# Loading and taking w1's last columns ahead of w3's in layer 0's feed-forward

## The chip, the cores and the metric

The kernel runs on one core of a Trainium2 chip. The metric is device time in microseconds, the median of three runs. Besides it there is one execution taken by the hardware profiler, whose rows are shown below; times in rows are microseconds from the start of that execution's span.

## The reference

Two identical layers in float32 on a batch of 4 tokens (one per sequence, width 512). Each layer is an attention block with a key and value cache and a gated feed-forward, both with a layernorm ahead and a residual add behind:

```python
x = x + A(layernorm(x), k_cache, v_cache, wq, wo)   # 32 query heads, 8 key/value heads, 4096 positions, width 128
x = x + B(layernorm(x), w1, w3, w2)

def B(x, w1, w3, w2):                # w1, w3: 512 x 1792, w2: 1792 x 512
    gate = x @ w1
    up = x @ w3
    return (silu(gate) * up) @ w2
```

Both layers use the same caches and weights. That is why so many bytes pass: the caches are loaded once per layer, less what is kept on chip between the layers.

## The kernel before, in words

All inputs lie in one array `rows` of 128 partitions, in the order in which they are used. On chip one large tile, `space`, holds everything loaded. It is divided into 218 places of 256 columns (1 KB per partition, 128 KB for the whole place). A list written out by hand, `LOADS` (line 54), gives every load: first place in the stream, number of places, place in `space`. The function `pump` (line 123) goes through that list in order. It issues a load only when all places of its destination are free, and stops at the first one that is not; `done` (line 158) frees a tile's places once the instructions that read it are written and calls `pump` again. So loads never overtake each other. All go out on SyncE (SP), whose queue is in order as well: at run time SP waits for the readers of the old tile, issues, and goes on to the next load. Each load is spread over the core's 16 DMA engines.

Layer 0 goes through the eight head groups in order and layer 1 in reverse, so that some tiles of the turn can be kept. For each group TensorE multiplies queries with keys (line 349), VectorE and ScalarE make the softmax, and TensorE multiplies with values (line 413). Then comes the feed-forward (function `feed_forward`, line 480).

There the columns are cut in two: "a" is the first 256 of each quarter, "b" the remaining 192. The weight tiles are w1a and w1b, w3a and w3b, each in four parts k = 0 to 3 (the contraction over 512 is cut into four). `part(bank, kind, ks)` (line 484) does the 16 matmuls of each of its parts as 4 per k and frees the part's tile behind them (w1 is not freed in layer 0, since layer 1 uses the loaded copy again). `swish` (line 504) is the sigmoid on ScalarE and a product on VectorE, `times_up` (line 508) the product with the other bank, `turn_h` (line 511) the transposes, `down` (line 528) the 14 tiles of w2. `hum` (line 496) issues filler matmuls on TensorE whose result is not used.

In layer 0 the places of these tiles are chained:

```
w3a      144 to 160        w1a   0 to 16         w1b  16 to 28
w3b 0    161 to 164        w3b 1 145 to 148      w3b 2 148 to 151     w3b 3 151 to 154
w2 0-1   154 to 158        w2 2-3 160 to 164     w2 4 158 to 160      w2 5-6 144 to 148
w2 7     148 to 150        w2 8-9 150 to 154
```

So w3b 0 needs room that a stored half tile frees (function `store_half`, line 213), w3b 1 to 3 need w3a's parts to be consumed, w2's second load (tiles 2 and 3) needs w3b 0 to be consumed, and the next ones w3a, w3b 1, w3b 2 and w3b 3.

Of the kernel before, what the change touches and what calls it, by code (L numbers as in the profile page):

```python
# [61 lines left out]
    (868, 8, 72), ("half", 0, 186), (876, 4, 188), (880, 8, 192), ("stash", 1, 202), (888, 8, 206),  # L62
# [15 lines left out]
def tile_decode_layers(ctx: ExitStack, tc: tile.TileContext, rows, out):  # L78
# [76 lines left out]
    def loaded(*key):  # L155
        return place(where[key], size[key[0]])

    def done(layer, *key):
        if layer == 0 and (key[0][:2] == "w1" or key[0] in ("wq", "wo") and key[1] >= HELD or key[:2] == ("kv", TURN) and key[2] in KEPT or key[0] == "w2" and key[1] >= LASTS):
            return  # L160
        at, n = where[key], size[key[0]]
        if key == CUT:
            half = where["half"]
            taken[half:half + n // 2] = [False] * (n // 2)
            at, n = at + n // 2, n // 2
        taken[at:at + n] = [False] * n
        pump()
# [18 lines left out]
    part = work.tile([P, 32], F32, name="part", tag="p", bufs=1)  # L186
# [33 lines left out]
    def scores():  # L220
        return psum.tile([P, BLOCK], F32, name="scores", tag="scores")
# [258 lines left out]
    def feed_forward(layer, xT, factor):  # L480
        gate, up = o_ps if layer else o_ps[::-1]
        cols = {"a": slice(0, HALF), "b": slice(HALF, FJ)}

        def part(bank, kind, ks=range(KC)):
            s = cols[kind[2]]
            for k in ks:
                w = loaded(kind, k).rearrange("p (j f) -> p j f", j=4)
                for j in range(4):
                    nc.tensor.matmul(bank[32 * j:32 * j + 32, s], xT[:, 32 * k:32 * k + 32], w[:, j],  # L489
                                     start=(k == 0), stop=(k == KC - 1))  # L490
                done(layer, kind, k)

        def old_x():
            nc.tensor.matmul(x_ps, ident, x_sb, start=True, stop=False)

        def hum(at, n):
            nc.tensor.matmul(pt[:, at:at + n, :], ident, ident.unsqueeze(1).to_broadcast([P, n, P]),
                             start=True, stop=True)

        h = work.tile([P, FJ], F32, name="h", tag="p", bufs=1)  # L500
        hT = work.tile([P, 14, B], F32, name="hT", tag="pT", bufs=1)
        pt = scores().rearrange("p (n s) -> p n s", n=NT)

        def swish(s):
            nc.scalar.activation(h[:, s], gate[:, s], AF.Sigmoid, scale=rstd[:, 0:1])
            nc.vector.scalar_tensor_tensor(h[:, s], gate[:, s], rstd[:, 0:1], h[:, s], op0=ALU.mult, op1=ALU.mult)

        def times_up(s):
            nc.vector.scalar_tensor_tensor(h[:, s], up[:, s], rstd[:, 0:1], h[:, s], op0=ALU.mult, op1=ALU.mult)

        def turn_h(u):
            if u == 0:
                for i in range(2):
                    nc.tensor.transpose(pt[:, i, :], h[:, i * P:(i + 1) * P], ident)
                nc.vector.tensor_copy(hT[:, 0:8, :],
                                      pt[:, 0:2, :].rearrange("p i (j b) -> p (i j) b", j=4)[:, :, 0:B])
            else:
                nc.tensor.transpose(pt[:, 2, :], h[:, 2 * P:3 * P], ident)
                nc.tensor.transpose(pt[:, 3, :], h[:, FJ - P:FJ], ident)
                nc.tensor.transpose(pt[0:64, 3, :], h[:, FJ - 64:FJ], ident)  # L520
                nc.vector.tensor_copy(hT[:, 8:12, :],
                                      pt[:, 2, :].rearrange("p (j b) -> p j b", j=4)[:, :, 0:B])
                last = pt[:, 3, :].rearrange("p (j u b) -> p j u b", j=2, u=2)
                for i in range(2):
                    nc.vector.tensor_copy(hT[64 * i:64 * i + 64, 12:14, :],
                                          last[64 * i:64 * i + 64, :, i, 0:B])

        def down():
            order = (*range(8), *range(LASTS, 14), *range(8, LASTS)) if layer else range(14)
            for n, m in enumerate(order):  # L530
                t = loaded("w2", m)
                for k in range(KC):
                    nc.tensor.matmul(x_ps[32 * k:32 * k + B, :], hT[:, m, :], t[:, k * P:(k + 1) * P],  # L533
                                     start=False, stop=(n == 13))
                done(layer, "w2", m)
                if layer == 0 and m in (1, 3, 8, 11):
                    hum(2 if m < 5 else 0, 1)
                if m == (1 if layer else 5):
                    turn_h(1)

        if layer == 0:
            part(up, "w3a", (0,))
            factor()
            part(up, "w3a", range(1, KC))
            old_x()
            hum(1, 3)
            part(gate, "w1a")
            part(up, "w3b", (0, 1))
            swish(cols["a"])
            times_up(cols["a"])  # L550
            hum(2, 2)
            turn_h(0)
            hum(2, 2)
            part(gate, "w1b")
            swish(cols["b"])
            nc.scalar.activation(spare, half[:, 0:1], AF.Exp)
            part(up, "w3b", (2, 3))
            times_up(cols["b"])
            hum(2, 1)
        else:  # L560
            old_x()
            part(gate, "w1a", (0,))
            factor()
            part(gate, "w1a", range(1, KC))
            part(gate, "w1b")
            swish(slice(0, FJ))
            part(up, "w3a")
            times_up(cols["a"])
            part(up, "w3b")
            turn_h(0)  # L570
            times_up(cols["b"])
        down()

    for layer in range(LAYERS):
# [54 lines left out]
        busy(BUSY[2])  # L629
        xT, factor = layernorm()  # L630
        feed_forward(layer, xT, factor)
    assert state['next'] == len(LOADS)
    nc.vector.tensor_copy(x_sb, x_ps)
# [47 lines left out]
```

## Time and profile before

| | |
|---|---|
| Median of three runs | 703.02 us (703.0 to 704.46) |
| Span of the profiled execution | 701.4 us, 1.6 us below that median |
| TensorE matmul busy | 421.4 us, 60% of the span |
| VectorE, ScalarE busy | 144.6 us (21%), 43.2 us (6%) |
| Moved by DMA | 297.34 MB, 424 GB/s over the span |
| DMA in the chain that ended last | 72% |

The profiled execution's own time is known by its span alone; 703.02 is the median of runs apart from it. In the page's slices of the span the DMA engines are at 9 tenths or more in 39 of 40. A DMA row counts an issue from where SP takes it up to where its instruction ends; the transfer itself comes later and is told by the time to landing. A landing is the moment at which all 16 engines have delivered their parts.

### The profile page before, as it was taken

To read this page: it belongs to the slowest core of one execution; us is meant where nothing else is said; L and a number is where in the kernel's file an instruction comes from. 1 tells how busy PE (TensorE), PEld (TensorE's weight loads), DVE (VectorE), ACT (ScalarE), POOL (GpSimd) and SP (SyncE) were. 2 spreads that over 40 slices of the span, in tenths; PEclk is the share of its full clock that TensorE was granted. 3 is DMA by queue.
4 is the path that set the end of the run, shared out by engine and by line. 5 is a ranking of instruction groups with operands and counts; after the bars stand their busy time and mean duration, and the time that the engine had idled before them with its cause. 6 is when DMAs were issued, how large, how long until landed. Compare 5 with 4: busy or idle time off the path is not lost.

```text
span 701.4 us, 7509 instructions
## 1 busy us (share of the span) xinstructions
PE 421.4 (60%) x3282; PEld 134.3 (19%) x3282; DVE 144.6 (21%) x512; ACT 43.2 (6%) x106; POOL 3.0 (0%) x10
## 2 busy tenths in 40 slices
PE   1266466644774529677687996544554725557677
PEld 0121121211221103121134231101111201112224
DVE  2012112121030203230221332102111401211322
ACT  0010000100000001010111210000100001000100
POOL 0000000000000000000000000000000000000000
PEclk9997677866698578886999998877867968778989
DMA  9999999999999999999999999999999999999996
GB/s 411 430 420 422 460 427 419 431 449 426 422 425 455 418 438 416 431 431 428 419 388 399 418 433 435 448 427 420 451 426 428 444 415 439 430 442 416 425 421 274
DMA packets 12847, 297.34 MB, mean 424 GB/s; under 512 B 1424, under 2 KB 1552, under 8 KB 4624
## 3 DMA queue, kind: packets, MB, share of 16 engines
q1 hardware_dynamic: 12816, 296.88, 98.9%
q8 instruction: 25, 0.41, 0.2%
q14 instruction: 6, 0.05, 0.0%
HBM read 296.81 MB, written 0.07 MB: 423 GB/s over the span
## 4 chain that ended last, share of the span: by engine, by line
DMA 72%; PE 24%; DVE 1%; another core or an unknown queue 1%; issue 1%; ACT 1%; SPq 1%; DVEq 0%; ACTq 0%
DMA space<-in_rows 72%; PE scores L349 12%; PE o L413 6%; PE sums_ps L330 1%; PE turned L374 1%; PE sums_ps L319 1%; PE o L489 1%; PE scores L230 0%; SPq L149 0%; ACT p L367 0%; DVE acc L361 0%; PE stored L467 0%; PE sums_ps L446 0%; PE sums_ps L457 0%
## 5 line engine op out<-in xcount | busy, mean ns | idle before, releaser
L349 PE MATMUL scores<-space,qT 128*32 128x512 f32 x1024 | 167.9, 712 | 137.6 <-DMA space<-in_rows 136.9
L413 PE MATMUL o<-space,pT 128*16 128x512 f32 x1024 | 152.5, 712 | 102.3 <-DMA space<-in_rows 92.0
L349 PEld LDWEIGHTS scores<-space,qT 128*32 128x32 f32 x1024 | 35.2, 122 | 213.6 <-issue 171.9
L413 PEld LDWEIGHTS o<-space,pT 128*16 128x16 f32 x1024 | 31.9, 109 | 201.2 <-issue 95.0
L361 DVE TENSOR_REDUCE acc<-scores 128x1 f32<-128x512 f32 x32 | 22.1, 691 | 184.8 <-PE scores L349 184.8
L367 ACT ACTIVATE p<-scores,acc 128x512 f32<-128x512 f32 x30 | 20.6, 687 | 557.2 <-DVE acc L361 420.4
L436 DVE SCALAR_TENSOR_TENSOR o<-o,acc,o 128x128 f32<-128x128 f32 x112 | 39.3, 351 | 44.4 <-PE o L413 41.0
L376 DVE COPY pT<-turned 128x256 f32<-128x256 f32 x32 | 13.6, 425 | 163.0 <-PE turned L374 163.0
L374 PE MATMUL turned<-ident,p 128*128 128x128 f32 x128 | 22.8, 305 | 11.3 <-ACT p L367 11.3
L374 PEld LDWEIGHTS turned<-ident,p 128*128 128x128 f32 x128 | 14.6, 150 | 45.2 <-ACT p L367 25.4
L319 PE MATMUL sums_ps<-space,xT 128*32 128x512 f32 x120 | 20.9, 718 | 2.7 <-DMA space<-in_rows 2.7
L447 DVE COPY o<-sums_ps 128x16 f32<-128x16 f32 x16 | 2.8, 174 | 93.0 <-PE sums_ps L446 93.0
L330 PEld LDWEIGHTS sums_ps<-same,shares 128*128 128x128 f32 x120 | 17.3, 222 | 16.9 <-DVE shares L325 11.9
L330 PE MATMUL sums_ps<-same,shares 128*128 128x4 f32 x120 | 18.6, 278 | 0.9 <-DVE shares L325 0.9
L489 PE MATMUL o<-space,xT 128*32 128x192 f32 (+1 forms) x256 | 13.5, 355 | 1.9 <-DVE xT L248 1.2
L467 PE MATMUL stored<-space,o 128*32 128x512 f32 x104 | 13.5, 592 | 0.0
L325 DVE TENSOR_SCALAR shares<-sums_ps,columns 128x512 f32<-128x512 f32 x15 | 11.1, 743 | 1.7 <-PE sums_ps L319 1.7
L533 PE MATMUL sums_ps<-space,hT 128*4 128x128 f32 x224 | 9.0, 273 | 3.8 <-DMA space<-in_rows 3.5
L235 PE MATMUL o<-columns,same 128*32 128x1 f32 x64 | 2.0, 181 | 14.5 <-DVE columns L579 13.5
L446 PEld LDWEIGHTS sums_ps<-columns,o 128*128 128x128 f32 x32 | 5.8, 227 | 19.9 <-issue 14.0
L489 PEld LDWEIGHTS o<-space,xT 128*32 128x32 f32 x256 | 7.5, 110 | 6.8 <-DVE xT L248 1.4
L446 PE MATMUL sums_ps<-columns,o 128*128 128x16 f32 x32 | 7.3, 306 | 0.6 <-DVE o L436 0.6
(105 smaller groups left out, 143.3 us busy)
## 6 DMA issues: line engine op xcount, KB each, us to landing
space<-in_rows SPq DMA_DIRECT2D x7, 4096.0 KB, 25.3
space<-in_rows SPq DMA_DIRECT2D x3, 6144.0 KB, 31.1
space<-in_rows SPq DMA_DIRECT2D x8, 2048.0 KB, 24.8
space<-in_rows SPq DMA_DIRECT2D x2, 7168.0 KB, 43.5
space<-in_rows SPq DMA_DIRECT2D x4, 3072.0 KB, 26.0
space<-in_rows SPq DMA_DIRECT2D x11, 1024.0 KB, 14.2
space<-in_rows SPq DMA_DIRECT2D x3, 3584.0 KB, 16.7
space<-in_rows SPq DMA_DIRECT2D x2, 5120.0 KB, 20.6
```

The costliest lines, as they stand in the source:

```text
L319: nc.tensor.matmul(wide[32 * k:32 * k + 32, :], xT[:, 32 * k:32 * k + 32], w[:, k, :], start=True, stop=True)
L330: nc.tensor.matmul(misc[:, h * B:(h + 1) * B], shares[:, h * DH:(h + 1) * DH], same[:, 0:B], start=True, stop=True)
L349: nc.tensor.matmul(ps[32 * b:32 * b + 32, :], qT[:, b, at:at + 32], u, start=(m < 2), stop=(m >= TILES - 2))
L361: nc.vector.tensor_reduce(acc[:, i:i + 1], ps, axis=AX.X, op=ALU.max, negate=True)
L367: nc.scalar.activation(p.rearrange("p n s -> p (n s)"), ps, AF.Exp, bias=acc[:, i:i + 1], scale=1.0 if scale is None else scale, accum_out ...
L374: nc.tensor.transpose(pt[:, n, :], p[:, n, :], ident)
L376: nc.vector.tensor_copy(pT, pt.rearrange("p n (b r) -> p n b r", b=B)[:, :, :, 0:ROW])
L413: nc.tensor.matmul(o_ps[i][32 * b:32 * b + ROW, :], pT[:, r // 2, b, :], t[:, j * NB * DH:(j + 1) * NB * DH], start=(r < 2), stop=(r >= TI ...
L436: nc.vector.scalar_tensor_tensor(o, o_ps[s][:, j * DH:(j + 1) * DH], acc[:, 16 + NB * s + j:17 + NB * s + j], o, op0=ALU.mult, op1=ALU.add)
L446: nc.tensor.matmul(misc[:, 0:B * REP], o, head, start=True, stop=True)
L467: nc.tensor.matmul(bank[32 * h:32 * h + 32, :], oT[:, h, :], w[:, h, :], start=first, stop=last)
L489: nc.tensor.matmul(bank[32 * j:32 * j + 32, s], xT[:, 32 * k:32 * k + 32], w[:, j], start=(k == 0), stop=(k == KC - 1))
```

## The change

Two things are moved, and no work is added or left out. In `LOADS` the load of w1b, (1168, 12, 16), moves ahead of those of w3b 0, (1196, 3, 161), and w3b 1, (1199, 3, 145). In layer 0's feed-forward the 16 matmuls on w3b 0 and 1 move from behind those on w1a to behind those on w1b, `swish` of the last columns and a small activation.

```diff
-    (1180, 16, 144), (1152, 16, 0), (1196, 3, 161), (1199, 3, 145), (1168, 12, 16), (1202, 3, 148), (1205, 3, 151),
+    (1180, 16, 144), (1152, 16, 0), (1168, 12, 16), (1196, 3, 161), (1199, 3, 145), (1202, 3, 148), (1205, 3, 151),
...
             part(gate, "w1a")
-            part(up, "w3b", (0, 1))
             swish(cols["a"])
             times_up(cols["a"])
             hum(2, 2)
...
             part(gate, "w1b")
             swish(cols["b"])
             nc.scalar.activation(spare, half[:, 0:1], AF.Exp)
+            part(up, "w3b", (0, 1))
             part(up, "w3b", (2, 3))
             times_up(cols["b"])
```

## Rows read from the trace of the kernel before

**Rows 1.** DMA queues on the page: packets, MB, share of 16 engines' span.

```profile
q1 hardware_dynamic: 12816, 296.88, 98.9%
q8 instruction: 25, 0.41, 0.2%
```

**Rows 2.** The chain that ended last: shares, then pieces (start, us, what).

```profile
DMA 72%; PE 24%; DVE 1%; another core or an unknown queue 1%; issue 1%; ACT 1%; SPq 1%; DVEq 0%; ACTq 0%
...
365.90 8.20 DMA space<-in_rows
...
375.77 6.79 DMA space<-in_rows
...
689.06 8.85 DMA space<-in_rows
```

**Rows 3.** Windows: busy PE, PEld, DVE, ACT, POOL; clock, DMA share, GB/s.

```profile
361.50:365.50 4.00, 3.19 (x54) 1.71 (x52) 1.02 (x7) 0.00 (x0) 0.55 (x1) 1.00 0.71 250
364.00:364.50 0.50, 0.50 (x16) 0.21 (x8) 0.00 (x0) 0.00 (x0) 0.44 (x1) 1.00 0.34 107
364.50:365.00 0.50, 0.50 (x10) 0.30 (x3) 0.00 (x0) 0.00 (x0) 0.00 (x0) 1.00 0.83 160
365.50:366.00 0.50, 0.50 (x6) 0.16 (x8) 0.00 (x0) 0.00 (x0) 0.00 (x0) 1.00 1.23 424
```

**Rows 4.** SP's issues: w1a, w3b 0, w3b 1, w1b, w2 2-3, 4, 7.

```profile
342.44 0.33 SPq L149 DMA_DIRECT2D space<-in_rows  x1
360.34 0.33 SPq L149 DMA_DIRECT2D space<-in_rows  x1
363.48 0.33 SPq L149 DMA_DIRECT2D space<-in_rows  x1
363.86 0.42 SPq L149 DMA_DIRECT2D space<-in_rows  x1
...
368.09 0.33 SPq L149 DMA_DIRECT2D space<-in_rows  x1
368.47 0.44 SPq L149 DMA_DIRECT2D space<-in_rows  x1
...
372.79 0.33 SPq L149 DMA_DIRECT2D space<-in_rows  x1
```

**Rows 5.** DMA view, us to landing: w1a, w3b 0, w3b 1, w1b, w2 2-3, 4.

```profile
space<-in_rows SPq DMA_DIRECT2D x1, 2048.0 KB, 22.7
space<-in_rows SPq DMA_DIRECT2D x1, 384.0 KB, 5.8
space<-in_rows SPq DMA_DIRECT2D x1, 384.0 KB, 3.7
space<-in_rows SPq DMA_DIRECT2D x1, 1536.0 KB, 7.0
space<-in_rows SPq DMA_DIRECT2D x1, 512.0 KB, 7.3
space<-in_rows SPq DMA_DIRECT2D x1, 256.0 KB, 8.2
```

**Rows 6.** A window at the kernel's end, columns as in rows 3.

```profile
695.50:696.00 0.50, 0.50 (x24) 0.49 (x21) 0.00 (x0) 0.00 (x0) 0.00 (x0) 1.00 0.64 225
```

**Rows 7.** TensorE's timeline: w3b 0-1, transposes, filler, w1b, w3b 2.

```profile
367.52 0.83 PE L489 MATMUL o<-space,xT 128*32 128x192 f32 x16
...
369.50 0.33 PE L514 MATMUL scores<-ident,h 128*128 128x128 f32 x1 [0.51 <-DVE h L509]
...
370.54 0.38 PE L497 MATMUL scores<-ident 128*128 128x256 f32 x1
370.91 1.51 PE L489 MATMUL o<-space,xT 128*32 128x192 f32 x32
...
372.23 0.51 PE L489 MATMUL o<-space,xT 128*32 128x192 f32 x8
```

**Rows 8.** DMA view of 374 to 376 us: packets, MB, share.

```profile
q8 instruction: 1, 0.02, 3.2%
```

## The prediction

> **What bounds the kernel now.** I read the page's shares first, then the chain of waits, then the stretch around the change by windows, the DMA issues there, and TensorE in order of time. The DMA engines' time on their one large queue is 98.9% of the span [rows 1], and 72% of the chain that ended last is loads [rows 2]. So the time is the time in which 16 engines move 296.9 MB. A gain must be DMA time that now stands idle; a loss must be DMA time that comes to stand idle.
>
> In the stretch of the change the engines are not full: from 361.5 to 365.5 us their mean share is 0.71, at 364.0 to 364.5 only 0.34 [rows 3]. The reader is to see why in the issues: w1a went out at 342.44, the next load, w3b 0, only at 360.34, w3b 1 only at 363.48, and w1b behind it at 363.86 [rows 4]. But the engines do not run dry together. w1a landed at 342.44 + 22.7 = 365.1 [rows 4, 5], after the window in which two thirds of the engine time went unused. So about 11 of 16 had by then finished their parts of w1a and w3b 0 and stood still, while about 5 were at work on them. A load has landed when its slowest part has, and the parts lie far apart: at the kernel's end, where nothing more is queued, the share is already 0.64 at 695.5 to 696.0, two us before the last landing at 689.06 + 8.85 = 697.9 [rows 2, 6]. The slowest engine hardly waited: w3b 0 landed at 366.1, w3b 1 at 367.2, w1b at 370.9 [rows 4, 5], w2's first load at 365.90 + 8.20 = 374.1 [rows 2], steadily one behind the other.
>
> **The change part by part.**
>
> *w1b's load goes out earlier.* By the code its room (places 16 to 28) was last held by tiles of the second and third head group, long consumed, so it follows w1a on SP: near 342.9 instead of 363.86. That puts 1536 KB, 370.9 - 367.2 = 3.7 us, more into the queue. w3b 0 and w3b 1 keep 360.34 and 363.48, because what frees their room is not moved. The fast engines then have work up to w2's first load, and the hole closes. It is worth (1 - 0.71) x 4.0 = 1.16 us of the mean engine [rows 3]. Only the order of the bytes changes: the seven loads from w1a to w2's first still land by 374.1.
>
> *TensorE's order.* The 16 matmuls on w3b 0 and 1 leave their place behind w1a, where they started from 367.52, and go behind w1b. Their going gains nothing: TensorE waited for VectorE's product of the first columns until 369.50 anyway, and that product hangs on w1a alone [rows 7]. w1b's matmuls began at 370.91, behind a filler that began at 370.54 [rows 7]; the filler hangs on that same chain, so an earlier landing can bring them forward by less than the 0.37 between the two, and nothing later waits for it. I take 0. Behind w1b then stand 24 instead of 8 matmuls ahead of w3b 3; 32 take 372.23 - 370.91 = 1.32, so 16 more cost 0.66. The down projection needs w2's first load, 374.1, and its first eight tiles hold only the first columns, so this lies beside the transfer.
>
> *Room that comes free later.* This is what the change adds. w2's second load goes into the room of w3b 0. It was issued at 368.09, 0.57 after the first matmul on w3b 0 (367.52) [rows 4, 7]. That matmul will start behind w1b's, at 372.23, so the load goes out near 372.8: 4.7 us later. The w2 loads behind it on SP (368.47 next, and 372.79, rows 4) follow at 0.4 to 0.5 us each, 0.38 as the closest pair of rows 4 shows. Until 372.8 nothing is queued behind w2's first load. So the hole is not closed but moved.
>
> *Its price.* Take an engine that runs dry in both orders. In the old one it stands still until w3b 1's data come (issue 363.48), in the new one until those of w2's second load (issue 372.8); the time from issue to data is in both and cancels. Between them lies the work from w3b 1 to w2's first load, which took the slowest engine 374.1 - 366.1 = 8.0 us. So it loses (372.8 - 363.48) - 8.0 = 1.3 us net; the closed hole is already counted in this. An engine that runs dry in neither loses 0. The slowest engine finishes w2's first load at 374.1, and new data come 1.0 to 2.0 us after an issue: w3b 1's brought the share to 0.83 from 364.5 on and the rate to 424 GB/s from 365.5 on [rows 3]. That is 373.8 to 374.8, so the slowest waits 0 to 0.7.
>
> By the mean: 11 of 16 engines x 1.3 = **+0.9 us**. The ends: -1.16 if the new hole costs nothing, 0 if the engine that ends last is one that never ran dry, +2.0 if it loses 1.3 and the 0.7 comes on top. I take +0.9, nearest to the 11 engines that rows 3 count.
>
> A lead matters, although only the slowest part counts, because instruction pages come over the same engines, 25 in all [rows 1], one of them in 374 to 376 [rows 8]. w2's second load landed at 368.09 + 7.3 = 375.4, the load behind it, 256 KB, at 368.47 + 8.2 = 376.7 [rows 4, 5]: 1.3 us for what takes 0.6 at w1b's rate. An engine with a lead pays such a stop out of it; without one, all wait.
>
> *Sum.* The profiled span is 701.4; the median of the runs, 703.02, lies 1.6 above. The span becomes 702.3 and the time 703.02 + 0.9 = **703.9**. Behind the feed-forward nothing is reordered. There w2's last load, issued at 375.77, landed 6.8 us later for some 1.3 us of transfer [rows 2], so 5 us are queued ahead and the shift should pass unaltered to the end, which again hangs on a load.
>
> **The rivals.**
>
> *The hole closes and the new one is free* (faster, inside the noise). For it: 0.34 in the resource that bounds [rows 3]. Against: nothing but w2's first load is queued up to 372.8. Price -1.16, time 701.9. The Trainium skill (Perfetto Trace Analysis, Identifying the Most-Contended Engine) says to find the gaps on the most contended engine and make what they wait for start sooner; that is this change, and by that rule the time is this rival's. The trace agrees that the gap is there.
>
> *It does nothing.* The engine that ends last is one of the 5 that never ran dry. Price 0, time 703.0. For it: the steady landings from 365.1 to 374.1.
>
> *The late w2 load stops the whole stage* (slower). It decides from the point where the data of w2's second load come after 374.1, when the slowest engine has nothing left either: the down projection waits, all engines start again together, and the page in 374 to 376 meets no lead at all. Price 0.7 + 1.3 = +2.0, time 705.0. For it: the 2.0 us until w3b 1's rate was full. Against: a share of 0.83 after 1.0 us. The Trainium skill (DMA: Bandwidth & Descriptors, Latency and other measured facts) gives about 0.6 us from issue to first byte on this kind of queue; by that the data would come at 373.4 and this rival falls away. The trace does not agree: 0.5 to 1.0 us after w3b 1's issue the share was still 0.34.
>
> **How the numbers follow.** A measurement of this kernel can tell about 0.2%, 1.4 us, from no change: faster is below 701.6, slower above 704.4. Chances: forecast 0.46, nothing 0.20, gain 0.11, whole stage 0.23. Faster: about half of the gain's chance, as 701.9 lies inside the bound: 0.06. Slower: nearly all of the whole stage (0.21) and a sixth of the forecast (0.08): 0.29. Same: 0.65. To leave out no more than 2 in 10 the range reaches over the forecast and nothing to most of the gain's upper half and to the whole stage's price: 702.3 to 705.0.
>
> **What would show it.** Right: w1b's issue directly behind w1a; a DMA share of 0.95 or more from 361.5 to 365.5; a new dip between 371 and 374.5; w2's second load issued at 372.6 to 373.0; w1b's matmuls still starting at 370.5 to 370.9; w2's last load landing 0.5 to 1.3 us after the old 382.6, and the kernel's last load later by about as much. Wrong: no new dip (the gain); a dip, but the same last landing (nothing); w2's second load landing after 376.5 and the last landing 2 us later (the whole stage). A second layer that starts later by more than the landings would make the whole account wrong.

## The result, and the profile after

The changed kernel took 705.29 us (median of 12 runs, 703.88 to 706.66), the kernel before 703.27 in the same runs (median of 12): a ratio of 1.0026, 95% interval 1.0016 to 1.0036. It is 2.0 us slower. The forecast was 703.9, its range ended at 705.0: wrong by 1.4 us. One execution of one kernel below (TensorE's order only, 722.14 us at a granted clock of 0.63 against 0.81 or more in the others) is left out of its ratio, and its trace is not read. The profiled execution of the changed kernel took 706.66, the slowest of the 12, so mainly its stretch around the change is laid beside the old one; its last landing, at 701.06 against 697.91, also holds two stops behind that stretch.

The page of the changed kernel, queues and first line of the chain, against [rows 1, 2]: loads still set the end, and the queue's share is a little lower.

```profile
q1 hardware_dynamic: 12816, 296.88, 98.6%
q8 instruction: 26, 0.43, 0.2%
...
DMA 69%; PE 27%; DVE 1%; another core or an unknown queue 1%; issue 1%; SPq 0%; ACT 0%; ACTq 0%; DVEq 0%
```

Windows of the changed kernel, columns as in [rows 3]; the last line is the kernel before, for the second of the new holes.

```profile
361.50:365.50 4.00, 3.19 (x48) 1.68 (x52) 0.80 (x5) 0.00 (x0) 0.55 (x1) 1.00 0.98 412
372.00:372.50 0.50, 0.50 (x20) 0.39 (x12) 0.11 (x1) 0.48 (x2) 0.00 (x0) 1.00 0.37 127
372.50:373.00 0.50, 0.47 (x16) 0.12 (x8) 0.31 (x1) 0.50 (x1) 0.00 (x0) 1.00 0.18 74
373.00:373.50 0.50, 0.50 (x9) 0.19 (x7) 0.02 (x1) 0.50 (x1) 0.00 (x0) 1.00 0.97 172
373.50:374.00 0.50, 0.33 (x2) 0.14 (x2) 0.40 (x1) 0.36 (x2) 0.00 (x0) 1.00 0.57 98
...
375.00:376.00 1.00, 0.24 (x6) 0.07 (x8) 0.00 (x0) 0.00 (x0) 0.00 (x0) 1.00 1.33 350
376.00:377.00 1.00, 1.00 (x22) 0.65 (x26) 0.00 (x0) 0.00 (x0) 0.00 (x0) 1.00 0.75 225
377.00:378.00 1.00, 0.30 (x8) 0.01 (x1) 0.00 (x0) 0.00 (x0) 0.00 (x0) 1.00 0.83 262
378.00:380.00 2.00, 0.17 (x5) 0.11 (x8) 0.00 (x0) 0.00 (x0) 0.00 (x0) 0.50 0.99 366
...
376.00:378.00 2.00, 0.88 (x14) 0.39 (x10) 0.00 (x0) 0.00 (x0) 0.00 (x0) 1.00 1.00 381
```

The old hole is closed (0.98 for 0.71), and there are two new ones. The first, from 371 on, was foretold. A window counts a packet whole where it starts, so a packet that takes long fills the window of its start and leaves the next one empty: the 0.97 from 373.0 to 373.5, at 172 GB/s, and the 1.33 from 375 to 376 come from such packets. By the packets' own times the engines are busy for 0.43 of 373.0 to 373.5, for 0.89 of 373.5 to 374.0 and for 0.98 and 0.93 of the two windows from 376 to 378. So the first hole is one in which engines stand still up to 373.2 and are then busy with packets that move little; the second, not foretold, is one in the rate alone (225 and 262 GB/s against 381). TensorE waits in it from 377.30 to 379.82, and in that wait, from 378 on, its granted clock is 0.50, the lower level.

SP's issues in the changed kernel: w1b, w3b 0, w3b 1, w2 2-3, w2 4, w2 5-6, w2's last, against [rows 4]; then the same loads (without w3b) in the DMA view, us from issue to landing, against [rows 5].

```profile
342.92 0.42 SPq L149 DMA_DIRECT2D space<-in_rows  x1
359.61 0.33 SPq L149 DMA_DIRECT2D space<-in_rows  x1
362.75 0.33 SPq L149 DMA_DIRECT2D space<-in_rows  x1
...
372.26 0.33 SPq L149 DMA_DIRECT2D space<-in_rows  x1
372.64 0.78 SPq L149 DMA_DIRECT2D space<-in_rows  x1
373.52 0.37 SPq L149 DMA_DIRECT2D space<-in_rows  x1
...
375.84 0.91 SPq L149 DMA_DIRECT2D space<-in_rows  x1
```

```profile
space<-in_rows SPq DMA_DIRECT2D x1, 1536.0 KB, 26.1
space<-in_rows SPq DMA_DIRECT2D x1, 512.0 KB, 3.6
space<-in_rows SPq DMA_DIRECT2D x1, 256.0 KB, 3.9
space<-in_rows SPq DMA_DIRECT2D x1, 512.0 KB, 6.3
space<-in_rows SPq DMA_DIRECT2D x1, 512.0 KB, 8.8
```

w2's second load landed at 372.26 + 3.6 = 375.9 (before 375.4), w2 5-6 at 373.52 + 6.3 = 379.8 (before 378.0), w2's last at 375.84 + 8.8 = 384.6 (before 382.6). So 0.5 us were lost at the first load of the restart and the rest, over 1.5, at the third, as far as the slowest of the 16 parts tells it.

TensorE's timeline in the changed kernel: the transposes, the filler, w1b and all of w3b as one row, and the wait for w2 5-6, against [rows 7]. The trace lists each of these float32 matmuls twice: the 16 on w3b 0 and 1 are 8 in the code, and one call of `hum` is two fillers.

```profile
369.01 0.44 PE L514 MATMUL scores<-ident,h 128*128 128x128 f32 x2 [1.08 <-DVE h L509]
369.74 0.70 PE L497 MATMUL scores<-ident 128*128 128x256 f32 x2 [0.28 <-DVE hT L515]
370.36 3.05 PE L489 MATMUL o<-space,xT 128*32 128x192 f32 x64
...
379.82 0.61 PE L533 MATMUL sums_ps<-space,hT 128*4 128x128 f32 x8 [2.52 <-DMA space<-in_rows]
```

### The profile page after: what moved, and what is told of

Its sections match the earlier page's. It is cut to its first block, busy times and chain, and to the rows that moved or that the text cites. A ratio compares the mean times of both kernels' runs of the same rounds, so it can differ in the third digit from the quotient of the medians.

```text
span 704.9 us, 7507 instructions
## 1 busy us (share of the span) xinstructions
PE 413.8 (59%) x3282; PEld 134.3 (19%) x3282; DVE 144.6 (21%) x512; ACT 43.2 (6%) x106; POOL 3.1 (0%) x10
## 4 chain that ended last, share of the span: by engine, by line
DMA 69%; PE 27%; DVE 1%; another core or an unknown queue 1%; issue 1%; SPq 0%; ACT 0%; ACTq 0%; DVEq 0%
DMA space<-in_rows 69%; PE o L413 14%; PE scores L349 7%; PE turned L374 1%; PE o L489 1%; PE sums_ps L330 1%; PE sums_ps L533 1%; DVE pT L376 1%; PE stored L275 1%; PE sums_ps L319 0%; SPq L149 0%; PE scores L497 0%; ACT p L367 0%; DVE o L436 0%
## 5 line engine op out<-in xcount | busy, mean ns | idle before, releaser
L349 PE MATMUL scores<-space,qT 128*32 128x512 f32 x1024 | 163.8, 695 | 141.7 <-DMA space<-in_rows 140.9
L413 PE MATMUL o<-space,pT 128*16 128x512 f32 x1024 | 149.2, 704 | 106.1 <-DMA space<-in_rows 99.9
L330 PEld LDWEIGHTS sums_ps<-same,shares 128*128 128x128 f32 x120 | 15.6, 204 | 16.2 <-DVE shares L325 11.1
L330 PE MATMUL sums_ps<-same,shares 128*128 128x4 f32 x120 | 16.9, 264 | 0.9 <-DVE shares L325 0.9
```

What stands on the lines that cost most here:

```text
L330: nc.tensor.matmul(misc[:, h * B:(h + 1) * B], shares[:, h * DH:(h + 1) * DH], same[:, 0:B], start=True, stop=True)
L349: nc.tensor.matmul(ps[32 * b:32 * b + 32, :], qT[:, b, at:at + 32], u, start=(m < 2), stop=(m >= TILES - 2))
L413: nc.tensor.matmul(o_ps[i][32 * b:32 * b + ROW, :], pT[:, r // 2, b, :], t[:, j * NB * DH:(j + 1) * NB * DH], start=(r < 2), stop=(r >= TI ...
```

## The experiments

The trace marks the landing of each of a load's 16 parts, one per engine. By these marks, in the kernel before, w2's first load came between 373.12 (the fastest engine) and 374.10 (the slowest); in the changed one between 370.64 and 374.09. So closing the old hole gave the fast engines 2.5 us and the slowest nothing. The next load, w2 2-3, came on all 16 within 0.56 us (375.32 to 375.89): the engines were nearly in step again, and none had a lead. The question was what sets the price of that restart. In this table the landing of w2's last load is the profiled execution's, and so is the last column: the mean of the 16 marks of the kernel's last load, against the kernel before (695.97).

| kernel | w2 2-3 issued | w2's last landed | median us | ratio (95%) | mean mark of the last load, us |
|---|---|---|---|---|---|
| before | 368.09 | 382.56 | 703.0 to 703.3 | | 0 |
| changed | 372.26 | 384.64 | 705.29 | 1.0026 (1.0016 to 1.0036) | +2.13 |
| loads only | 370.35 | 385.07 | 706.45 | 1.0038 (1.0023 to 1.0052) | +2.92 |
| TensorE's order only | | | 706.14 | 1.0033 (1.0021 to 1.0045) | |
| ready loads first | 372.08 | 381.78 | 704.43 | 1.0011 (1.0003 to 1.0020) | +0.89 |
| fillers in the wait | 372.12 | 383.78 | 704.95 | 1.0021 (1.0011 to 1.0032) | +1.26 |
| half of w1b early | 368.69 | 382.65 | 703.21 | 0.9985 (0.9971 to 0.9998) | -0.09 |
| w3b 0 first | 370.79 | 382.67 | 703.52 | 0.9997 (0.9985 to 1.0009) | -0.07 |
| later | 373.42 | 383.90 | 705.47 | 1.0022 (1.0011 to 1.0034) | +1.89 |
| merged | 372.68 | 382.86 | 703.83 | 1.0001 (0.9990 to 1.0013) | +0.80 |
| merged, later | 373.53 | 383.54 | 704.65 | 1.0017 (1.0009 to 1.0026) | +1.59 |
| split | 372.13 | 384.31 | 706.51 | 1.0046 (1.0034 to 1.0058) | +2.55 |
| w3b 0 first, merged | 370.86 | 382.24 | 703.15 | 0.9999 (0.9991 to 1.0008) | -0.16 |
| both of w3b first | 370.86 | 382.44 | 703.52 | 1.0012 (1.0001 to 1.0023) | +0.20 |

The landing of w2's last load does not put the kernels in the order of their medians: split landed earlier than the changed kernel and took longer. The last column does, but for neighbours within 0.3 us of each other. A landing is the slowest engine's, and single stops move it: in the changed kernel it lies 1.5 to 3.6 us behind the old one from one load to the next behind the stretch. The mean of the 16 lies 2.1 to 2.2 us behind at every load from 393 us on. It is of one trace for each kernel.

**Each half of the change alone.** The kernel before with only the list of loads changed:

```diff
-... (1152, 16, 0), (1196, 3, 161), (1199, 3, 145), (1168, 12, 16), (1202, 3, 148), ...
+... (1152, 16, 0), (1168, 12, 16), (1196, 3, 161), (1199, 3, 145), (1202, 3, 148), ...
```

> Only the load of w1b is moved ahead; TensorE takes w3b 0 and 1 at their old place, behind w1a. Theory 1 (the loss is the time for which w2's second load waits for w3b 0 to be consumed): w3b 0 now lands near 370.0, is consumed at once, and w2's second load goes out near 370.6 instead of 372.3, so the fast engines stand still for some 1 us instead of 3: -0.5 to +0.5 us against the kernel before. Theory 2 (the loss is TensorE's clock, which fell to half while it waited for w2): no long wait, no fall, -0.5 to +0.5. Theory 3 (w1b's earlier load by itself disturbs what follows): as the changed kernel, +1.8.

And the changed kernel with the old list, so that only TensorE's order is new:

> Only the 16 matmuls on w3b 0 and 1 are moved behind those on w1b; the loads keep their old order. Theory 1: w2's second load is issued near 372.3, with the old hole at 361.5 to 365.5 besides; the leads of the engines are lost either way, so +1.5 to +2.5 us, as much as the whole change or a little more. Theory 2: +1.8 if the clock falls in the same stretch. Theory 3: within 0.3 of the kernel before, since the loads are not moved.

706.45 and 706.14: either half alone is as slow as both, or slower. For the loads alone theories 1 and 2 had said -0.5 to +0.5, and it came out 3.2 us slower. There TensorE takes w3b 0 and 1 at their old place, ahead of the transposes, and waits for them. Its timeline, and one window of the same kernel:

```profile
369.76 0.53 PE L489 MATMUL o<-space,xT 128*32 128x192 f32 x8 [2.69 <-DMA space<-in_rows]
...
374.29 3.95 PE L489 MATMUL o<-space,xT 128*32 128x192 f32 x48
```

```profile
376.00:378.00 2.00, 2.00 (x32) 1.07 (x24) 0.40 (x1) 0.84 (x2) 0.00 (x0) 0.50 0.04 16
```

The matmuls on w1b and on w3b 2 and 3 then run at the clock's lower level (48 in 3.95 us, where the changed kernel takes 64 in 3.05) and end at 378.2, w3b 2's room comes free late, w2 7 goes out only at 377.76, and next to nothing moves from 376 to 378 (0.04). The hole had gone to another load of the same chain of rooms, and here the clock had its part in it. Of the second kernel only the times are used.

**Loads that need no room go first.** The changed kernel, with w2 12-13 and w2 4, whose places are free, put ahead of w2 2-3:

```diff
-... (1208, 4, 154), (1212, 4, 160), (1216, 2, 158), ... (1230, 2, 156), (1232, 4, 28), ...
+... (1208, 4, 154), (1232, 4, 28), (1216, 2, 158), (1212, 4, 160), ... (1230, 2, 156), ...
```

> The whole change, and two loads of w2 whose room is free anyway (tiles 12 and 13, and tile 4; 0.79 MB, 1.9 us) go out ahead of the second load, which waits. Theory 1: the slowest engine has work up to 376.0, the fastest to 372.5, data of the second load come near 373.5; the hole is nearly gone, and the time falls by 1.5 to 3 us against the changed kernel: -1.2 to +0.3 against the one before. Theory 2: tiles 2 and 3 land later (near 377), TensorE waits as long and the clock falls all the same: +1 to +2. Theory 3: +1.8.

704.43: the first hole is filled (w2's last landed 2.9 us earlier than with the change alone), yet only 0.9 us of it reach the end. The loads behind wait for places of w2 tiles that the down projection frees; w2 2-3 now lands later, TensorE waits for it, and a window of this kernel shows the hole again, further on:

```profile
380.00:382.00 2.00, 2.00 (x31) 1.03 (x31) 0.41 (x3) 0.00 (x0) 0.00 (x0) 0.63 0.78 262
```

**The clock.** The changed kernel, with four calls of `hum` (eight filler matmuls as the trace counts them) in TensorE's wait:

```diff
+                if layer == 0 and m == 4:
+                    for _ in range(4):
+                        hum(2, 2)
```

> The whole change, and 8 more filler matmuls (2.6 us) behind w2's tile 4, where TensorE waited 2.5 us in the changed kernel and its granted clock fell to 0.5 until 385. Theory 1: the clock stays at 1.0 there, the second layer starts some 0.5 us earlier, but the landings are the same and the time is within 0.4 of the changed kernel (+1.4 to +2.2 against the one before). Theory 2: most of the loss goes with the fall of the clock: 0 to +0.8 against the one before.

Two windows of this kernel: the granted clock stays 1.00, and the low rate from 376 on is there all the same.

```profile
376.00:378.00 2.00, 1.26 (x23) 0.63 (x16) 0.00 (x0) 0.00 (x0) 0.00 (x0) 1.00 0.87 305
378.00:380.00 2.00, 2.00 (x16) 1.36 (x15) 0.00 (x0) 0.00 (x0) 0.00 (x0) 1.00 1.01 376
```

704.95, against 705.29 for the change alone; the two are not told apart by their intervals. So most of the loss is there without the clock's fall. Some of it may be the clock's: on the mean of the 16 marks this kernel is 1.43 us late at w2's last load and 1.26 at the kernel's last, the changed one 1.76 and 2.13. The loads' losses fell otherwise here: w2 4, issued 3.2 us ahead of its turn (of the moment at which the load ahead of it had landed), lost 1.1 on the slowest engine, and w2 5-6, 3.9 ahead, 0.5.

**Half of w1b early.** The kernel before, w1b in two loads, the second at w1b's old place; TensorE's order is the old one:

```diff
-... (1152, 16, 0), (1196, 3, 161), (1199, 3, 145), (1168, 12, 16), (1202, 3, 148), ...
+... (1152, 16, 0), (1168, 6, 16), (1196, 3, 161), (1199, 3, 145), (1174, 6, 22), (1202, 3, 148), ...
```

> The kernel before, with the first half of w1b (0.79 MB, 1.9 us) loaded ahead of w3b 0 and the second half at its old place; TensorE's order stays. Theory 1 (what counts is the time from which the queue holds nothing and the time at which w3b 0 is consumed): the hole at 361.5 to 365.5 is half closed, w3b 0 and 1 land near 368.0 and 368.9, so they are consumed at most 0.6 us later and w2's second load goes out near 368.6, before anything runs dry; TensorE waits about 0.5 us, too short for its clock. -1.2 to +0.2 us against the kernel before. Theory 3 (an earlier load of w1b disturbs by itself): +0.5 to +2.

A window, SP's issue of w2 2-3, and its time to landing in this kernel:

```profile
361.50:365.50 4.00, 3.24 (x48) 1.71 (x52) 0.74 (x5) 0.00 (x0) 0.55 (x1) 1.00 0.98 392
```

```profile
368.69 0.33 SPq L149 DMA_DIRECT2D space<-in_rows  x1
```

```profile
space<-in_rows SPq DMA_DIRECT2D x1, 512.0 KB, 6.7
```

The old hole is closed as in the changed kernel (0.98), and w2 2-3 still goes out early. Here closing the hole can be seen alone: w2's first load landed at 374.15 against 374.10 before, and w2 2-3 at 375.4 in both. The median is 703.21, against 703.33 for the kernel before in the same runs. The ratio, 0.9985, has an interval that just leaves 1 out, the one version of which that is so; single runs of the kernel before reached 707.85 there. So w1b's early load does no harm, and the closed hole is worth 0.1 us by the medians and 1 at most. On the mean of the 16 marks it gave 1.31 us at w2's first load; of that 0.61 were left at w2's last and 0.1 at the kernel's last load. The lead that it gives the fast engines is not kept.

**The room freed 1.5 us earlier.** The changed kernel, w3b 0 taken ahead of w1b:

```diff
+            part(up, "w3b", (0,))
             part(gate, "w1b")
...
-            part(up, "w3b", (0, 1))
+            part(up, "w3b", (1,))
```

> The whole change, but TensorE takes w3b 0 ahead of w1b (both have landed by then) and w3b 1 behind it, so w2's second load can go out near 370.8 instead of 372.3. Theory 1: the queue is empty for 1.5 us less; -0.8 to -2 us against the changed kernel, that is 0 to +1.0 against the one before. If the price does not hang on that time but on the small loads that restart the queue, it is as the changed kernel, +1.5 to +2.

703.52, the loss is gone but for 0.2: it hangs on when w3b 0's room comes free. w2 2-3 goes out at 370.79, 3.2 us ahead of its turn on the slowest engine (374.0), and loses 0.1 there; w2 5-6, 3.6 us ahead of its turn, loses 0.9.

**The room freed 1.2 us later.** The changed kernel, four more filler matmuls ahead of w3b 0:

```diff
+            hum(2, 2)
+            hum(2, 2)
             part(up, "w3b", (0, 1))
```

> The whole change, with two pairs of filler matmuls (1.3 us at full clock) ahead of those on w3b 0 and 1, so that w2's second load goes out near 373.6 instead of 372.3; the down projection starts 0.5 us later. Theory 1: every engine stands still 1.3 us longer, +1.0 to +1.6 us against the changed kernel, +2.8 to +3.4 against the one before. If the price is that of a restart, whenever it comes: +1.5 to +2.2 against the one before.

705.47, no more than with the change alone. Two windows of this kernel:

```profile
374.00:375.00 1.00, 1.00 (x24) 0.61 (x18) 0.42 (x1) 0.00 (x0) 0.00 (x0) 1.00 0.80 78
376.00:378.00 2.00, 0.75 (x16) 0.35 (x16) 0.00 (x0) 0.00 (x0) 0.00 (x0) 0.87 1.04 408
```

The first hole is longer, and at its end the engines move 78 GB/s at a share of 0.80; but the second is not there (1.04, 408 GB/s). By the packets' own times the engines are busy for 0.49 of 374 to 375, the rest of the 0.80 reaches beyond. On the mean of the 16 marks w2 2-3 came 2.07 us late, against 0.76 in the changed kernel, and the loads behind added nothing to it. Here w2 5-6 was issued 0.53 behind w2 4 and 3.5 us ahead of its turn; in the changed kernel 0.88 behind and 376.5 - 373.5 = 3.0 ahead. So a price that grows with the lateness of the first load alone was refuted: the loads behind it count. (The fillers are two calls of `hum`.)

**One larger load.** The changed kernel, w2 2-3 and w2 4 in one load of 768 KB:

```diff
-... (1212, 4, 160), (1216, 2, 158), ...
+... (1212, 6, 158), ...
```

> The whole change, with w2's second and third load (tiles 2, 3 and 4) as one DMA of 0.79 MB into the same six places. In the changed kernel the third and fourth load behind the empty queue landed 1.2 to 2.1 us later than their size explains. If this comes from several small loads restarting an empty queue one by one, the single larger one saves 0.5 to 1.5 us against the changed kernel. If it comes only from the late issue of the first, the time stays within 0.4 of the changed kernel, +1.4 to +2.2 against the one before.

703.83, although it was issued 0.4 us later than in the changed kernel. A window of this kernel, and the merged load and w2 5-6 in the DMA view:

```profile
376.00:378.00 2.00, 0.98 (x20) 0.64 (x23) 0.00 (x0) 0.00 (x0) 0.00 (x0) 1.00 1.00 400
```

```profile
space<-in_rows SPq DMA_DIRECT2D x1, 768.0 KB, 4.3
space<-in_rows SPq DMA_DIRECT2D x1, 512.0 KB, 5.2
```

The second hole is gone, and TensorE's clock stays at its higher level there. The load carries 1.8 us instead of 1.25, so w2 5-6 was issued 3.9 us ahead of its turn.

The new theory: a load needs some 3 to 4 us between its issue and its turn on an engine; what it lacks, the engine stands still or is busy with slow packets; and after a hole the second and third load lack it too, when the loads ahead of them are small. Four kernels tested it against a fixed price per hole.

**Merged, and later.** The two edits just shown, together.

> The one larger load of w2 2-4, and besides two fillers ahead of w3b 0, so that its room comes free about 1.1 us later (issue near 373.8 instead of 372.7). Theory A, what is lost is what each load lacks of some 3 us between its issue and its turn on the slowest engine: the larger load now lacks 1.1 more and nothing else changes; w2's last lands near 384.0 instead of 382.9, median about 704.9. Theory B, a hole has one price and its length does not matter: as with the larger load alone, 703.8, w2's last near 382.9. Theory C, the price is the clock, which falls when TensorE waits long enough: 705.3 or more, with the clock at 0.5 for some us.

704.65: 0.8 more than merged alone (1.1 by the two ratios) for 0.85 us more lateness (373.53 against 372.68). By the last column of the table it is 0.79. With the loads behind it supplied, the price does grow with the lateness. The clock fell as well (0.54 from 378 to 380), so part may be its.

**Split.** The changed kernel, w2 2-3 as two loads of 256 KB:

```diff
-... (1212, 4, 160), (1216, 2, 158), ...
+... (1212, 2, 160), (1214, 2, 162), (1216, 2, 158), ...
```

> The changed kernel with w2 2-3 as two loads of 256 KB, both waiting for w3b 0. Theory A (each load needs its own lead): the two small ones carry 0.65 us each, so the loads behind them have no more lead than before and there is one more to stop at; 705.3 to 706.3, and packets of 4 KB that take over 0.5 us again at the loads behind the first. Theory B (one price per hole): 705.3, no change. If the number of issues on SP sets it, each 0.4 us: 705.7.

706.51, slower again than the change alone, and above the value expected. (On the slowest engine w2's last landed 0.3 us earlier than in the changed kernel; on the mean of the 16 it came 0.3 later, and the kernel's last load 0.4.) A window of this kernel, and the four loads from w2 2 to w2 5-6 in the DMA view:

```profile
376.00:378.00 2.00, 0.63 (x14) 0.33 (x10) 0.00 (x0) 0.00 (x0) 0.00 (x0) 1.00 0.95 272
```

```profile
space<-in_rows SPq DMA_DIRECT2D x1, 256.0 KB, 2.8
space<-in_rows SPq DMA_DIRECT2D x1, 256.0 KB, 3.2
space<-in_rows SPq DMA_DIRECT2D x1, 256.0 KB, 4.6
space<-in_rows SPq DMA_DIRECT2D x1, 512.0 KB, 5.4
```

The first small load is there sooner (2.8 us), and w2 4, issued 2.4 us ahead of its turn, pays: it landed 2.2 us behind the load ahead of it, for 0.65 us of transfer. The Trainium skill (Perfetto Trace Analysis, DMA Optimizations) says that where DMA engines are generally idle, smaller transfers may let the whole end sooner. Here they are idle in the hole alone; the first part came sooner and the kernel's end later.

**w3b 0 first, and merged.** Both edits on the changed kernel.

> w3b 0 taken ahead of w1b, and w2 2-4 as one load. Theory A: the load goes out near 370.8, some 3.2 us ahead of its turn at 374.0, and carries 1.9 us, so that w2 5-6 behind it (372.4) has 3.5 us of lead as well; the 0.96 us that stood at w2 5-6 with w3b 0 first alone goes; w2's last near 381.8, median 702.3 to 703.0. Theory B (one price per hole, and there is still a hole on the fast engines): 703.5.

703.15, 0.15 above theory A's upper end and 0.35 under theory B's value: as fast as the kernel before, not faster.

**Both of w3b ahead of w1b.** The changed kernel with `part(up, "w3b", (0, 1))` moved there.

> w3b 0 and w3b 1 both taken ahead of w1b, loads as in the changed kernel. w3b 1 lands at 370.8, so TensorE waits some 0.3 us for it, and w2 5-6's room comes free near 371.0 instead of 372.4. Theory A: w2 5-6 then has 4 us of lead and loses nothing; w2's last near 381.8, median 702.4 to 703.1. Theory B: as with w3b 0 first alone, 703.5. If the wait for w3b 1 holds back w3b 2 and 3 and with them w2 7 and 8: 704 or more.

703.52, the value of the fixed price: the theory's 702.4 to 703.1 missed. w2 5-6 lost nothing, as foretold, but w2 2-3, issued at 370.86 and 3.2 us ahead of its turn, came 0.7 late on one engine, the slowest. That is most likely no want of lead. By the packet records an instruction page passed from 373.39 to 374.27, and one engine trails the next by 0.64 from then on; the page at 374.32 in the kernel before left one engine 0.67 behind in the same way. So this trace does not show that the theory missed for want of a lead at w2 2-3. That a lead between 3 and 4 us does not always do, and that what a load loses there is not a fixed number, rests on w3b 0 first and on the fillers in the wait.

## Why the prediction was wrong

*Right:* w1b directly behind w1a (342.92); the old hole closed (0.98); the new dip from 371 to 374.5; w2's second load late by 4.2 us (372.26; 372.8 was foretold, since w1b's matmuls came 0.55 us earlier, not under 0.37); no loss at the first columns; and the sign.

*The step that failed* is the price: "By the mean: 11 of 16 engines x 1.3 = **+0.9 us**". That is the price of w2's second load alone; the loads behind it, said only to "follow at 0.4 to 0.5 us each", have no term. For the one load the sum came near. On the mean of the 16 marks w2's first load came 1.38 us earlier than in the kernel before (the closed hole, counted at 1.16) and w2 2-3 came 0.76 later (counted at 0.9). "The time from issue to data is in both and cancels" held for engines that stood still: less the 8 packets of its transfer, the first part landed 1.64 us after the issue at w3b 1 (366.09 - 363.48 - 0.97) and 1.79 at w2 2-3 (375.32 - 372.26 - 1.27). Then came what the sum lacks. At w2 5-6 the mean was 1.55 us late, at w2's last load 1.76, and from the load that landed at 398.50 in the kernel before up to the last one 2.1 to 2.2. The median rose by 2.0.

*On the slowest engine* the closed hole brought nothing (374.10, 374.09 and, closed alone, 374.15). "The slowest waits 0 to 0.7" was right in size, about 0.5 at w2 2-3, but it was no wait: 13 engines had run dry, while the last three went straight on from w2's first load to the next one, at 373.52 to 373.66, with first packets of 0.50 to 0.56 us where the steady stream has 0.159. Then w2 5-6 landed 3.26 us behind w2 4 for 1.25 us of transfer, 2.0 lost. From w2's first load to its last it took 10.55 us instead of 8.46, in which the old order has a page's stop of 0.7 that the new one's hole swallowed: +2.1. "The shift should pass unaltered to the end" was right from 398 us on; before that the mean lost 0.4 more. The kernel with the fillers, whose clock stayed up, lost nothing there, but one trace of each does not show the cause.

*The mean* was thus a fair measure of the loss, as the table's last column shows, and a poor one of the gain: the lead of the fast engines was spent again, in this kernel at once and with half of w1b early by the end.

*The rows had it.* In [rows 3] the window 364.5 to 365.0 has a share of 0.83 at 160 GB/s. I read it as "data after 1.0 us". Beside 250 GB/s at 0.71 it says that the engines were busy with slow packets: by the packet records those of w3b 1, 3 KB each, took up to 0.69 us there and 0.121 in the steady stream. In the changed kernel a packet of 4 KB takes 0.159 us in the steady stream, up to 0.91 at the restart from 373.2, and up to 1.97 where w2 5-6 begins.

*The rivals.* "The late w2 load stops the whole stage", 705.0, had nearly the right shape and the right time within 0.3 us: all parts of w2 2-3 landed after 374.1 and within 0.56 us. Its first packets began earlier, at 373.22. Its second half was to be a page that meets no lead; the page came in the hole, at 372.0, and w2 5-6 took its place. Its chance, 0.23, was too low and the forecast's 0.46 too high: its ground against it was the misread share. The Trainium skill's 0.6 us to the first byte (DMA: Bandwidth & Descriptors, Latency and other measured facts), which would have dropped this rival, is near what the trace shows: the first packet began 0.96 us after the issue began and 0.63 after it ended. But the first of the 16 parts landed 3.1 us after the issue, and a first byte is not a landing. Another page of it gives a price for the whole transfer (SBUF — State Buffer, The DMA setup-cost knee): some 2 us for any transfer besides its bytes at 436 GB/s. Worked out from it, as an estimate, 256, 512 and 768 KB take 2.6, 3.2 and 3.8 us; the first load of the restart took 2.8, 3.6 and 4.3, so the trace agrees but for 0.2 to 0.5 us more. "It does nothing" and the free hole are refuted for the change as a whole; for the closed hole alone the first is what the landings show. The rule quoted for the free hole, to find the gaps and make what they wait for start sooner (it stands under Optimization Strategy on its page), gained 0.1 us by the medians where only the gap was closed.

*Open:* why w2 5-6 with 3.0 us of lead lost 2.0 while w2 4 with 3.2 lost nothing (and, in the other kernels, loads with 3.2 to 3.9 us lost 0.5 to 1.1 three times and otherwise next to nothing), so that the lead alone does not tell the loss; and what makes the first packets of a late load slow; no run here separates the reading of memory from the queue's own work.

## What to carry to other kernels

A hole in the mean DMA share is not yet time to be gained: look whether landings already follow one behind the other through it, as here, where closing it alone gave the fast engines a lead that was spent again. Whoever moves a load ahead of others in a full queue must follow what its consumer's place does to the rooms, and must price, besides the load that restarts an empty queue, the two or three behind it (here leads of 2.4 to 3.9 us from issue to turn were at times too little and at times enough). Where that cannot be avoided, one larger load restarted cheaper in these runs than several small ones. To read a loss of some tenths from one trace, compare the mean of a late load's 16 marks; its landing can lie a microsecond off by one engine's stop.

## What the runs showed of the hardware

DMA engines can be busy and move little: by the packets' own times 0.89 at 129 GB/s from 373.5 to 374.0 and 0.98 at 229 from 376 to 377 in the changed kernel, against 1.03 at 408 from 376 to 378 in the kernel with the room freed later. The 16 engines finish the parts of one load up to 3.5 us apart for seven loads on end, and one hole that stops 13 of them brings them within 0.6 us. An instruction page on its way left one engine 0.67 us behind the next in the kernel before, and most likely the 0.64 with both of w3b first.
